# Expert loop of a routed layer: branch hints for TensorE, and the second tile behind the third and later ones

## Chip, cores and metric

The kernel runs on one core of one Trainium2 chip. The metric is the device time of one execution in microseconds (us). TensorE (PE) multiplies; its weight loads are listed as PEld, and the profile puts the steps of its sequencer there too, as PEldq. VectorE is DVE, ScalarE ACT, GpSimd POOL, SyncE SP.

## The reference

Three layers follow each other on 3072 tokens: an attention with a window of 16 and block sums, a dense gated layer `((x @ w1) * (x @ w2)) @ w3 @ w_out`, and a routed layer, which the change is about:

```python
skip_score = x @ w_skip
do_compute = skip_score > 0
out = x.copy()
xc = x[do_compute]
logits = xc @ w_gate                       # 8 experts
e_idx = np.argmax(logits, axis=1)
gate_w = probs[np.arange(len(xc)), e_idx]  # softmax of the chosen one
for e in range(E):
    mask = e_idx == e
    h = np.maximum(xc[mask] @ w1[e], 0.0)  # 512 x 1024
    y[mask] = gate_w[mask, None] * (h @ w2[e])
out[do_compute] = xc + y
```

How many tokens an expert gets is known only at run time. The inputs here give experts 0 to 7 the counts 266, 41, 394, 201, 29, 63, 212 and 100.

## The kernel before

Attention and the dense layer fill the span up to about 655 us, and the router writes, beside them, a list of token numbers for each expert and the number of tiles of 128 tokens. The expert stage then runs `Experts.run` (L845): the experts are unrolled in the program, and for each the number of tiles `ns[e]` decides by branches which of its code is run. All five engines carry the same branches; the order inside a block is the order in which the code is written.

One tile is `compute` (L765): 24 matmuls for the hidden layer (`hmul`, two halves of 12), relu on ScalarE, eight transposes (`hturn`), 24 matmuls for the output (`ymul`), a scaling and addition on VectorE (`eo`) and a scatter on GpSimd. Products are made from a high and a low part of each operand, so a tile's rows have to be gathered (`gather`, GpSimd), turned by TensorE (`turn`, four transposes) and split by ScalarE (`xh`, high) and VectorE (`xl`, low) before `hmul` can start. This is done ahead, inside the tile before: the argument `turns` names the slots that are turned in the middle of the tile, ahead of its last 12 matmuls, and at its end. Slots 0 and 2 take the first tile of the even and the odd experts by turns, 1 and 3 the second (`own`), 4 the third, 5 the fourth; `nxt` is the next expert's first. In the trace the slots' buffers are all named xg, exh and exl; the order of instructions keeps numbers: xg_7303, 7307, 8648, 8652, 8656 and 8660 are slots 0 to 5.

Inside `compute`, `other()` also casts pieces of the next expert's weights (`piece`: high part on ScalarE, L734, low part on VectorE, L737), 16 pieces an expert: `HALF` spreads 8 over a tile, `CUTS` 16. The pieces come from seven buffers (eraw); when one is free, SyncE loads the next 512 KB into it (L718).

An expert with more than one tile goes through the true part of `tc.If(ns[e] > 1)`: first and second tile (`second`), then `rest`, which is nested: a third tile if there are more than two, a fourth if more than three, a loop for any further one. Where a branch is not taken, a short block makes up for the counts of the semaphores that the skipped code would have raised; on TensorE it waits until all earlier matmuls are done. An expert with one tile goes through the else part. The code of each part stands in this order: first and second tile, third, fourth, loop, those short blocks, else part; a jump leads over what is not run. Expert 0's first tile is ahead of its branch, and expert 7 has no else part.

Of the kernel before, what the change touches and what calls it, by code (L numbers as in the profile page):

```python
# [52 lines left out]
PE = ET.PE  # L53
PIECES = "a"
RMORE = 3
CUTS0 = (0, 1, 1, 1, 2, 3)
ELOAD = 16
CUTS = (4, 3, 1, 2, 3, 3)
HALF = (2, 1, 0, 1, 2, 2)
# [3 lines left out]
class Attention:  # L63
# [60 lines left out]
    def sum(self, i):  # L124
        nc = self.nc
        vt = self.sums.pop(i)
        sm = self.pool.tile([4 * NBLK, D], F32, tag="sm", name="sm", bufs=2)
        for n in (8, 4, 2):
            nc.vector.tensor_add(vt[:, 0:n, :], vt[:, 0:n, :], vt[:, n : 2 * n, :])
        nc.vector.tensor_add(sm, vt[:, 0, :], vt[:, 1, :])  # L130
        self.sums["half", i] = sm
        if i % 2:
            nc.vector.tensor_add(sm, self.sums.pop(("half", i - 1)), self.sums.pop(("half", i)))
            nc.vector.tensor_scalar_mul(self.vs[:, i // 4, i // 2 % 2, :], sm, 1.0 / 32.0)
# [225 lines left out]
def split(nc, hi, lo, src):  # L360
    nc.scalar.activation(hi, src, AF.Copy)
    nc.vector.tensor_sub(lo, src, hi.bitcast(F32))  # L362
# [309 lines left out]
class Experts:  # L672
# [92 lines left out]
    def compute(self, col, e, slot, turns=(None, None), cuts=()):  # L765
        nc, pool, ps = self.nc, self.pool, self.ps
        (ah, al), (bh, bl) = self.a[e % 2], self.b[e % 2]
        xg, xh, xl = self.xg[slot], self.xh[slot], self.xl[slot]
        hrs, ths = [], []
        hps = [ps.tile([P, 512], F32, tag="h", name="hp", bufs=2) for _ in range(2)]  # L770
        cuts = list(cuts)

        def other():
            for _ in range(cuts.pop(0) if cuts else 0):
                self.piece(PIECES)

        def hmul(s, lo, hi):
            fs = slice(s * 512, s * 512 + 512)
            for q in range(lo, hi):
                c, j = divmod(q, 3)  # L780
                l, r = ((xh, ah), (xh, al), (xl, ah))[j]
                nc.tensor.matmul(hps[s], l[:, c, :], r[c][:, fs], start=(q == 0), stop=(q == 11))  # L782

        def relu(s):
            hr = pool.tile([P, 512], F32, tag="hr", name="hr", bufs=2)
            nc.scalar.activation(hr, hps[s], AF.Relu)  # L786
            hrs.append(hr)

        def hturn(s):
            tp = ps.tile([P, 4, P], F32, tag="ht", name="htp", bufs=2)  # L790
            for c in range(4):
                nc.tensor.transpose(tp[:, c, :], hrs[s][:, c * P : (c + 1) * P], self.ident)
            th = pool.tile([P, 4, P], F32R, tag="th", name="hth", bufs=2)
            tl = pool.tile([P, 4, P], F32R, tag="tl", name="htl", bufs=2)
            split(nc, th, tl, tp)
            ths.append((th, tl))

        yp = ps.tile([P, 512], F32, tag="y", name="yp", bufs=2)

        def ymul(s, lo, hi):  # L800
            th, tl = ths[s]
            for q in range(lo, hi):
                c, j = divmod(q, 3)
                f = 4 * s + c
                l, r = ((th, bh), (th, bl), (tl, bh))[j]
                nc.tensor.matmul(
                    yp, l[:, c, :], r[f], start=(f == 0 and j == 0), stop=(f == 7 and j == 2)
                )

        hmul(0, 0, 12)  # L810
        other()
        relu(0)
        hmul(1, 0, 6)
        other()
        hturn(0)
        other()
        hmul(1, 6, 12)
        relu(1)
        if turns[0] is not None:
            self.turn(turns[0], ps)  # L820
        other()
        ymul(0, 0, 6)
        hturn(1)
        other()
        ymul(0, 6, 12)
        if turns[1] is not None:
            self.turn(turns[1], ps)
        other()
        ymul(1, 0, 12)
        if turns[2:]:  # L830
            self.turn(turns[2], ps)
        o = pool.tile([P, DM], F32, tag="o", name="eo", bufs=2)
        nc.vector.scalar_tensor_tensor(
            out=o, in0=yp, scalar=xg[:, DM : DM + 1], in1=xg[:, 0:DM], op0=ALU.mult, op1=ALU.add
        )
        nc.gpsimd.indirect_dma_start(  # L836
            out=self.out,
            out_offset=bass.IndirectOffsetOnAxis(ap=col, axis=0),
            in_=o,
            in_offset=None,  # L840
            bounds_check=N - 1,
            oob_is_err=False,
        )

    def run(self, pool, ps, early):  # L845
        tc, nc = self.tc, self.nc
        self.pool, self.ps = pool, ps
        cj = pool.tile([P, 1], I32, name="cj")
        manual = lambda: tc.manual_schedule(engines=ENGINES)
        with tc.If(early < P):  # L850
            with manual():
                self.gather(self.col(0, 0), 0)
                self.turn(0, ps)
        with tc.If(early < 2 * P):
            with manual():
                self.gather(self.col(0, 1), 1)
        def state():
            return self.done, self.loaded, dict(self.raws), list(self.free)

        def rest(e, p):  # L860

            with tc.If(ns[e] > 2):  # L862
                with manual():
                    self.compute(self.col(e, 2), e, 4, (5, None))
                with tc.If(ns[e] > 3):  # L865
                    with manual():
                        self.compute(self.col(e, 3), e, 5)
                    with tc.If(ns[e] > 4):  # L868
                        with tc.For_i(4, ns[e], 1) as j:
                            nc.vector.tensor_copy(cj, self.idx[:, bass.ds(j + e * NTILE, 1)])  # L870
                            self.gather(cj, 4)
                            self.turn(4, ps)
                            self.compute(cj, e, 4)

        def second(e, p, cuts=()):
            self.gather(self.col(e, 3), 5)
            self.compute(self.col(e, 1), e, (1, 3)[p], (4, None), cuts)

        ns = None
        for e in range(E):  # L880
            p = e % 2
            more = e + 1 < E
            own, nxt = (1, 3)[p], (2, 0)[p] if more else None
            with manual():
                if more:
                    self.gather(self.col(e + 1, 0), (2, 0)[p])
                self.gather(self.col(e, 2), 4)
                if more:
                    self.gather(self.col(e + 1, 1), (3, 1)[p])
                if e == 0:  # L890
                    self.compute(self.col(0, 0), 0, 0, (None, 1, nxt), CUTS0)
                elif not more:
                    self.compute(self.col(e, 0), e, (0, 2)[p], (own, None))
            if ns is None:
                ns = [nc.values_load(self.nt[0:1, z : z + 1], min_val=0, max_val=NTILE) for z in range(E)]  # L895
            if not more:
                with tc.If(ns[e] > 1):
                    with manual():
                        second(e, p)
                    rest(e, p)  # L900
                continue


            before = state()
            with tc.If(ns[e] > 1) as many:  # L905
                with manual():
                    if e:
                        self.compute(self.col(e, 0), e, (0, 2)[p], (own, nxt), HALF)
                    second(e, p, HALF)
                rest(e, p)  # L910
            after = state()
            self.done, self.loaded, self.raws, self.free = before[0], before[1], dict(before[2]), list(before[3])
            with many.Else():
                with manual():
                    if e:
                        self.compute(self.col(e, 0), e, (0, 2)[p], (None, nxt), CUTS)
                    else:
                        for _ in range(sum(HALF)):
                            self.piece(PIECES)
            now = state()  # L920
            assert now[:2] == after[:2] and list(now[2]) == list(after[2])
            assert [id(t) for t in now[3]] == [id(t) for t in after[3]]
# [251 lines left out]
```

## Time and profile before

| | |
|---|---|
| median of 3 runs | 875.9 us (875.15 to 879.59) |
| profiled execution | 877.2 us |
| its span, first to last instruction | 875.4 us |
| TensorE busy in the span | 821.2 us (94%) |
| VectorE, ScalarE, GpSimd busy | 513.4, 466.0, 99.3 us |
| mean granted clock of TensorE | 0.984 |
| packets of the instruction fetch (queue q8) | 64, together 1.05 MB |

The span is cut into 40 slices of 21.9 us; the expert stage fills the last ten. [...] An idle time in brackets stands ahead of an instruction and names what ended it; "issue" is a wait for nothing that the profile shows. It is counted from the end of the instruction before, which is modelled for matmuls. Branches, loads of a register and event waits of a sequencer are not counted as busy time, but have their own rows by source line.

### The profile page before, as it was taken

The page shows a single profiled execution, that of the slowest core. Times are in us where ns is not written, and L with a number is a line of the kernel's source. Part 1 is how long each engine was busy: PE and PEld are TensorE (multiplying, and loading weights), DVE is VectorE, ACT ScalarE, POOL GpSimd, SP SyncE. Part 2 cuts the span into 40 slices and gives each one's busy share as a digit, 9 for nine tenths or more (in the row PEclk, how much of TensorE's full clock was granted, in tenths as well). Part 3 has the DMA queues.
Part 4 walks back from the last instruction along what each step waited for, and adds up shares of the span by engine and source line. Part 5 has one row for each costly group of instructions (what it writes and reads, how often), then busy time and mean ns, then how long its engine had stood idle before and what let it go on. Part 6 is the DMA issues. An engine that isn't in the chain of part 4 may idle for free. (4 is left out here: it accounts for less than half of the span.)

```text
span 875.4 us, 17512 instructions
## 1 busy us (share of the span) xinstructions
PE 821.2 (94%) x6478; PEld 766.4 (88%) x6478; DVE 513.4 (59%) x1663; ACT 466.0 (53%) x1230; POOL 99.3 (11%) x135
## 2 busy tenths in 40 slices
PE   3988889999999999999999999999999799996996
PEld 3988879999999999999999998999998687784684
DVE  5888888876555546457535456633435365254861
ACT  5777988775663444455434446522426364254761
POOL 2000000000001100010001000210214121022321
PEclk9999999999999999999999999999999999997999
DMA  7959965542522423215212212710326376045920
GB/s 209 236 168 207 225 167 174 148 100 59 130 56 74 116 73 89 57 35 123 73 37 62 58 49 67 242 50 1 104 96 245 111 225 209 13 137 166 306 80 21
DMA packets 124612, 105.02 MB, mean 120 GB/s; under 512 B 92914, under 2 KB 98082, under 8 KB 124496
## 3 DMA queue, kind: packets, MB, share of 16 engines
q1 hardware_dynamic: 120144, 98.04, 40.2%
q0 software_dynamic: 4352, 5.51, 2.1%
q8 instruction: 64, 1.05, 0.5%
q14 instruction: 52, 0.43, 0.2%
HBM read 90.45 MB, written 16.64 MB: 122 GB/s over the span
## 5 line engine op out<-in xcount | busy, mean ns | idle before, releaser
L547 PE MATMUL x2p<-wh,slab 128*128 128x266 f32 (+1 forms) x768 | 156.1, 290 | 0.0
L547 PEld LDWEIGHTS x2p<-wh,slab 128*128 128x128 f32 x768 | 124.2, 189 | 0.8
L547 PE MATMUL x2p<-wl,slab 128*128 128x256 f32 (+1 forms) x384 | 108.9, 284 | 0.0
L200 ACT ACTIVATE pr<-pr,st 128x120 f32<-128x120 f32 x192 | 73.4, 384 | 34.5 <-DVE st L190 34.2
L526 DVE TENSOR_TENSOR a<-a,ab 128x256 f32<-128x256 f32 x84 | 35.2, 419 | 76.5 <-ACT a L517 76.0
L504 PE MATMUL ab<-slab,wA1h 128*128 128x256 f32 x384 | 72.4, 286 | 0.5 <-DVE slab L362 0.5
L547 PEld LDWEIGHTS x2p<-wl,slab 128*128 128x128 f32 x384 | 72.8, 190 | 0.0
L504 PE MATMUL ab<-slab,wB1h 128*128 128x256 f32 x384 | 72.5, 287 | 0.0
L517 ACT ACTIVATE a<-ab 128x256 f32<-128x256 f32 x96 | 36.3, 378 | 65.7 <-PE ab L504 62.0
L504 PE MATMUL ab<-slab,wB2h 128*128 128x256 f32 x384 | 70.7, 282 | 0.0
L504 PE MATMUL ab<-slab,wA2h 128*128 128x256 f32 x384 | 70.6, 282 | 0.0
L527 ACT ACTIVATE slab<-a 128x256 fp32r<-128x256 f32 x84 | 35.0, 417 | 63.6 <-DVE a L526 63.1
L504 PEld LDWEIGHTS ab<-slab,wA1h 128*128 128x128 f32 x384 | 59.0, 189 | 1.1 <-DVE slab L362 0.7
L504 PEld LDWEIGHTS ab<-slab,wB1h 128*128 128x128 f32 x384 | 58.9, 190 | 0.4
L504 PEld LDWEIGHTS ab<-slab,wB2h 128*128 128x128 f32 x384 | 59.1, 190 | 0.0
L504 PEld LDWEIGHTS ab<-slab,wA2h 128*128 128x128 f32 x384 | 59.1, 189 | 0.0
L528 DVE TENSOR_TENSOR slab<-a,slab 128x256 fp32r<-128x256 f32 x84 | 36.1, 430 | 38.7 <-ACT slab L527 38.2
L178 PE MATMUL sp<-kaug,qblk 128*128 128x120 f32 x384 | 53.1, 284 | 4.6 <-issue 2.9
L786 ACT ACTIVATE hr<-hp 128x512 f32<-128x512 f32 x30 | 17.9, 598 | 71.1 <-PE hp L782 71.0
L504 PE MATMUL ab<-slab,wA2l 128*128 128x256 f32 x192 | 54.1, 282 | 0.0
L504 PE MATMUL ab<-slab,wA1l 128*128 128x256 f32 x192 | 54.1, 282 | 0.0
L504 PE MATMUL ab<-slab,wB2l 128*128 128x256 f32 x192 | 53.9, 281 | 0.0
(178 smaller groups left out, 2134.5 us busy)
## 6 DMA issues: line engine op xcount, KB each, us to landing
eraw<-in_moe_w SPq DMA_DIRECT2D x64, 512.0 KB
raw<-in_moe_w SPq DMA_DIRECT2D x32, 512.0 KB
vaug<-in_v SPq DMA_DIRECT2D x32, 240.0 KB
x2e<-row SPq DMA_DIRECT2D x24, 256.5 KB
vt<-in_v SPq DMA_DIRECT2D x16, 384.0 KB
kn<-in_k SPq DMA_DIRECT2D x32, 192.0 KB
qn<-in_q SPq DMA_DIRECT2D x32, 192.0 KB
out<-row SPq DMA_DIRECT2D x24, 256.0 KB
```

The costliest lines, as they stand in the source:

```text
L178: self.nc.tensor.matmul(sp[:, i, 0:KA], self.qblk[:, t, :, :], self.kaug[:, t, :], start=True, stop=True)
L200: nc.scalar.activation(pr[:, i, :], pr[:, i, :], AF.Exp, scale=-1.0, bias=st[:, 0, i : i + 1], accum_out=st[:, 1, i : i + 1],)
L504: self.nc.tensor.matmul(pp[:, s, :], l[:, c, fs], r[:, c, :], start=(c == 0 and j == 0), stop=(c == 3 and j == 2),)
L517: nc.scalar.activation(a, pp[:, 0, :], AF.Copy)
L526: nc.vector.tensor_mul(a, a, pp[:, 1, :])
L527: nc.scalar.activation(gh[:, f % 4, :], a, AF.Copy)
L528: nc.vector.tensor_sub(gl[:, f % 4, :], a, gh[:, f % 4, :].bitcast(F32))
L547: self.nc.tensor.matmul(po[:, 0 : hi - lo], l[:, f, s * P : s * P + P], r[:, 4 * h + f, lo:hi], start=(h == 0 and f == 0 and j == 0), stop ...
L786: nc.scalar.activation(hr, hps[s], AF.Relu)
```

## The change

Three things change. First, four branches of each expert carry labels, and `soon` places a hint on TensorE (a register step that compares `ns`, and the hint) at the start of a tile: at the start of the first tile for the branch behind it, at the third for the next, at the fourth for the next, and at an expert's last tile for the first branch of the next expert. For expert 0 the hint for its second branch stands right ahead of that branch. Second, in the true part the second tile is computed behind `rest`, hence after the third and later ones; slot 4 is turned in the first tile already (for experts 1 to 7 in the place of the next expert's turn, which moves to the tile's end; for expert 0 at the very end), and the gather of the fourth tile comes ahead of the first. Third, expert 7 gets the same form as the others, with an else part.

```diff
--- before.py
+++ after.py
@@ -827,8 +827,9 @@
             self.turn(turns[1], ps)
         other()
         ymul(1, 0, 12)
-        if turns[2:]:
-            self.turn(turns[2], ps)
+        for slot in turns[2:]:
+            if slot is not None:
+                self.turn(slot, ps)
         o = pool.tile([P, DM], F32, tag="o", name="eo", bufs=2)
         nc.vector.scalar_tensor_tensor(
             out=o, in0=yp, scalar=xg[:, DM : DM + 1], in1=xg[:, 0:DM], op0=ALU.mult, op1=ALU.add
@@ -857,24 +858,26 @@
         def state():
             return self.done, self.loaded, dict(self.raws), list(self.free)
-        def rest(e, p):
-
-            with tc.If(ns[e] > 2):
+        def soon(label, n, least):
+
+            tc.mark_branch_hint_location(label, hint=n >= least, engines=[PE])
+
+        def rest(e):
+
+            with tc.If(ns[e] > 2, label=f"three{e}"):
                 with manual():
+                    soon(f"four{e}", ns[e], 4)
                     self.compute(self.col(e, 2), e, 4, (5, None))
-                with tc.If(ns[e] > 3):
+                with tc.If(ns[e] > 3, label=f"four{e}"):
                     with manual():
+                        soon(f"five{e}", ns[e], 5)
                         self.compute(self.col(e, 3), e, 5)
-                    with tc.If(ns[e] > 4):
+                    with tc.If(ns[e] > 4, label=f"five{e}"):
                         with tc.For_i(4, ns[e], 1) as j:
                             nc.vector.tensor_copy(cj, self.idx[:, bass.ds(j + e * NTILE, 1)])
                             self.gather(cj, 4)
                             self.turn(4, ps)
                             self.compute(cj, e, 4)
-
-        def second(e, p, cuts=()):
-            self.gather(self.col(e, 3), 5)
-            self.compute(self.col(e, 1), e, (1, 3)[p], (4, None), cuts)
         ns = None
         for e in range(E):
@@ -888,32 +891,33 @@
                 if more:
                     self.gather(self.col(e + 1, 1), (3, 1)[p])
                 if e == 0:
-                    self.compute(self.col(0, 0), 0, 0, (None, 1, nxt), CUTS0)
-                elif not more:
-                    self.compute(self.col(e, 0), e, (0, 2)[p], (own, None))
+                    self.compute(self.col(0, 0), 0, 0, (None, 1, nxt, 4), CUTS0)
             if ns is None:
                 ns = [nc.values_load(self.nt[0:1, z : z + 1], min_val=0, max_val=NTILE) for z in range(E)]
-            if not more:
-                with tc.If(ns[e] > 1):
-                    with manual():
-                        second(e, p)
-                    rest(e, p)
-                continue
+            half, whole = (HALF, CUTS) if more else ((), ())
+
             before = state()
-            with tc.If(ns[e] > 1) as many:
+            with tc.If(ns[e] > 1, label=f"two{e}") as many:
                 with manual():
+                    soon(f"three{e}", ns[e], 3)
+                    self.gather(self.col(e, 3), 5)
                     if e:
-                        self.compute(self.col(e, 0), e, (0, 2)[p], (own, nxt), HALF)
-                    second(e, p, HALF)
-                rest(e, p)
+                        self.compute(self.col(e, 0), e, (0, 2)[p], (own, 4, nxt), half)
+                rest(e)
+                with manual():
+                    if more:
+                        soon(f"two{e + 1}", ns[e + 1], 2)
+                    self.compute(self.col(e, 1), e, own, (None, None), half)
             after = state()
             self.done, self.loaded, self.raws, self.free = before[0], before[1], dict(before[2]), list(before[3])
             with many.Else():
                 with manual():
+                    if more:
+                        soon(f"two{e + 1}", ns[e + 1], 2)
                     if e:
-                        self.compute(self.col(e, 0), e, (0, 2)[p], (None, nxt), CUTS)
+                        self.compute(self.col(e, 0), e, (0, 2)[p], (None, nxt), whole)
                     else:
                         for _ in range(sum(HALF)):
                             self.piece(PIECES)
```

Expert 0's branches on TensorE; xg_8648 is the next expert's first tile, xg_8656 and exh_8657 the third tile's slot 4 (a piece of the difference):

```order
 L762 MATMUL xt<-ident,xg_8648 128x128 x4
-L895 TENSOR_LOAD nt
-L905 COMPARE_AND_BRANCH
+L762 MATMUL xt<-ident,xg_8656 128x128 x4
+L896 TENSOR_LOAD nt x2
+L902 COMPARE_AND_BRANCH
+L863 REGISTER_ALU
+L1174 BRANCH_PREFETCH_HINT
+L867 COMPARE_AND_BRANCH
+L863 REGISTER_ALU
+L1174 BRANCH_PREFETCH_HINT
+L782 MATMUL hp<-ea0h,exh_8657 128x512
```

The turn of slot 4 has moved to the end of the first tile, and behind the two branches the third tile comes first.

TensorE from expert 0's last tile to expert 1's first, before; L868, L865 and L862 are the short blocks of the branches not taken, exh_8649 is expert 1's first tile:

```order
L868 UNCONDITIONAL_BRANCH
L865 UNCONDITIONAL_BRANCH
L862 UNCONDITIONAL_BRANCH
L905 UNCONDITIONAL_BRANCH
L895 TENSOR_LOAD nt
L905 COMPARE_AND_BRANCH
L782 MATMUL hp<-ea1h,exh_8649 128x512
```

The same place after the change, first up to the second tile of expert 0 (exh_7308):

```order
L875 UNCONDITIONAL_BRANCH
L871 UNCONDITIONAL_BRANCH
L867 UNCONDITIONAL_BRANCH
L863 REGISTER_ALU
L1174 BRANCH_PREFETCH_HINT
L782 MATMUL hp<-ea0h,exh_7308 128x512
```

and, behind that tile's matmuls, up to expert 1's first:

```order
L902 UNCONDITIONAL_BRANCH
L863 REGISTER_ALU
L1174 BRANCH_PREFETCH_HINT
L902 UNCONDITIONAL_BRANCH
L896 TENSOR_LOAD nt
L902 COMPARE_AND_BRANCH
L863 REGISTER_ALU
L1174 BRANCH_PREFETCH_HINT
L782 MATMUL hp<-ea1h,exh_8649 128x512
```

The second tile now stands between the short blocks and the next expert's branch.

ScalarE at the start of expert 1's true part, as it is for all experts from 1 to 6, before; ea0h is the next expert's first weight, hr the relu:

```order
L905 COMPARE_AND_BRANCH
L734 ACTIVATE ea0h<-eraw_7312 128x512 x2
L786 ACTIVATE hr<-hp 128x512
L734 ACTIVATE ea0h<-eraw_7313 128x512
L361 ACTIVATE hth<-htp 128x512
```

and after, where wA1h belongs to the next expert's second weight:

```order
L902 COMPARE_AND_BRANCH
L734 ACTIVATE ea0h<-eraw_7312 128x512 x2
L734 ACTIVATE wA1h<-eraw_8665 128x512 x2
L786 ACTIVATE hr<-hp 128x512
L734 ACTIVATE ea0h<-eraw_7313 128x512
L361 ACTIVATE hth<-htp 128x512
```

Two casts of the second weight, which stood in the second tile, have moved ahead of the first tile's relu.

## Rows read from the trace of the kernel before

**Rows 1.** The page: granted clock of TensorE in 40 slices, in tenths.
```profile
PEclk9999999999999999999999999999999999997999
```
**Rows 2.** Timeline of TensorE: start, duration (us), engine, line, operation, count [idle before].
```profile
681.32 0.39 PE L782 MATMUL hp<-ea0h,exh 128*128 128x512 f32 x1
...
698.30 0.77 PE L782 MATMUL hp<-ea1h,exh 128*128 128x512 f32 x1 [4.38 <-issue]
...
765.25 0.49 PE L782 MATMUL hp<-ea1h,exh 128*128 128x512 f32 x1 [1.03 <-ACT ea0h L734]
...
798.45 0.77 PE L782 MATMUL hp<-ea0h,exh 128*128 128x512 f32 x1 [7.48 <-issue]
...
815.21 0.47 PE L782 MATMUL hp<-ea1h,exh 128*128 128x512 f32 x1 [1.47 <-ACT ea0h L734]
...
855.54 0.50 PE L782 MATMUL hp<-ea1h,exh 128*128 128x512 f32 x1 [1.05 <-PEq L862]
```
**Rows 3.** TensorE's sequencer by source line, cut by stretches: count, ns min/median/max, first and last start.
```profile
L905 PEldq COMPARE_BRANCH  x1: 3377/3377/3377, 694.8 to 694.8; - x1
L868 PEldq COMPARE_BRANCH  x2: 181/264/347, 761.5 to 764.5; - x2
L868 PEldq EVENT_SEMAPHORE  x1: 51/51/51, 764.3 to 764.3; - x1
L895 PEldq TENSOR_LOAD <-nt x1: 302/302/302, 764.7 to 764.7; - x1
L862 PEldq COMPARE_BRANCH  x2: 181/2190/4199, 788.2 to 792.7; - x2
L905 PEldq COMPARE_BRANCH  x1: 4988/4988/4988, 793.3 to 793.3; - x1
L905 PEldq COMPARE_BRANCH  x1: 4012/4012/4012, 811.0 to 811.0; - x1
L862 PEldq COMPARE_BRANCH  x2: 193/1764/3334, 851.7 to 855.3; - x2
```
**Rows 4.** Queue q8: packets, MB, share; whole span, 788.2 to 798.3, 713.7 to 764.
```profile
q8 instruction: 64, 1.05, 0.5%
q8 instruction: 3, 0.05, 2.2%
q8 instruction: 3, 0.05, 0.4%
```
**Rows 5.** Stretches: us, PE, PEld, DVE, ACT, POOL busy, granted clock, DMA share, GB/s.
```profile
655.80:660.09 4.29, 4.29 (x18) 3.43 (x19) 0.00 (x0) 1.12 (x2) 2.94 (x5) 1.00 0.35 126
698.30:705.28 6.98, 6.98 (x18) 5.46 (x19) 0.58 (x2) 1.43 (x3) 2.06 (x2) 0.57 0.61 191
798.45:804.91 6.46, 6.46 (x18) 5.05 (x19) 0.00 (x0) 1.14 (x3) 0.00 (x0) 0.63 0.23 80
```
**Rows 6.** Timeline, all engines, end of expert 0's first tile.
```profile
668.38 0.60 PE L762 MATMUL xt<-ident,xg 128*128 128x128 f32 x4
668.74 0.48 PE L782 MATMUL hp<-ea0h,exh 128*128 128x512 f32 x1
669.02 0.60 ACT L361 ACTIVATE exh<-xt 128x512 fp32r<-128x512 f32 x1 [1.07 <-PE xt L762]
669.65 0.69 DVE L362 TENSOR_TENSOR exl<-xt,exh 128x512 fp32r<-128x512 f32 x1 [0.72 <-ACT exh L361]
```
**Rows 7.** Timeline of GpSimd and TensorE, expert 2's first tile: gather of slot 4, next expert's turn.
```profile
719.19 1.00 POOL L749 DMA_INDIRECT xg<-x2e,idx  x1 [0.30 <-issue]
723.76 0.66 PE L762 MATMUL xt<-ident,xg 128*128 128x128 f32 x4 [0.23 <-DMA xg<-x2e,idx]
```
**Rows 8.** Expert 5's tile: VectorE's busy time, granted clock; and SyncE's loads around it.
```profile
815.21:828.89 13.68, 11.43 (x20) 1.00 0.93 317
809.47 22.20 SPq L718 DMA_DIRECT2D eraw<-in_moe_w  x13
```

## The prediction

> **What bounds the kernel now.** I read the page first: TensorE's granted clock is 0.9 or more in every slice of the span but one, near 790 to 810 us [rows 1]. Its timeline then shows why: TensorE stands still there. In the expert stage (15 tiles; the inputs give experts 0 to 7 the counts 3, 1, 4, 2, 1, 1, 2, 1) it is fed almost without a break inside a tile, and its timeline has five seams between experts, with the idle time in brackets [rows 2]: 4.38 us before expert 1, 1.03 before expert 3, 7.48 before 4, 1.47 before 5, 1.05 before 7. Together 15.4 us; only this can be won.
>
> What ends these waits is TensorE's own sequencer [rows 3]. A short jump (at 761.5, over the unused loop of expert 2) takes 0.35 us. The long ones take 3.38 us (694.8, into expert 1's else part), 4.20 (788.2, over expert 3's unused tiles), 4.99 (793.3, into expert 4's else part), 4.01 (811.0, expert 5's) and 3.33 (851.7, over expert 6's unused tiles). While two of them run, from 788.2 to 798.3, the queue of the instruction fetch moves three packets; 64 of them make 1.05 MB, so one is 16 KB [rows 4]. A long jump waits for code.
>
> Part of such a wait is hidden. The sequencer reached the jump at 811.0, and TensorE ran dry at 815.21 - 1.47 = 813.74: a lead of 2.7 us. Before experts 1 and 4 the lead was lost for a second reason. After a branch not taken, the sequencer waits until TensorE is empty (the event at 764.3, where the last matmul's end is 765.25 - 1.03 = 764.22), and the next long jump comes only then, with nothing left to hide it.
>
> The two long seams cost more than their idle time [rows 5]. [...] Expert 5, after 1.47 us of idling, kept full clock [rows 8].
>
> **Part by part: what is removed.** Each long jump that is taken now has a hint one tile earlier, that is some 12.5 us ahead of a fetch of 3.3 to 5.0. And the second tile now stands behind the branches of the third and later ones, so that the emptying of TensorE comes inside an expert, and the jump into the next expert has its lead back. If the hints fetch as they say, the five seams go: 15.4 us. The idle times that remain are of the size of expert 5's, which left the clock alone, so 2.69 + 2.17 = 4.9 us go with them. Expert 7 loses the turn of its unused second tile (the else part asks for none): a turn in the stream takes 668.74 - 668.38 = 0.36 us [rows 6]. Sum 20.7.
>
> **What is added or moved.**
> Emptying: experts 0, 2, 3 and 6 have two or more tiles and leave the branches early, so four times TensorE empties ahead of the second tile. The nearest row is the seam before expert 3, whose jump was short: 1.03 us. Of that the load of the count, 0.30, moves away, behind the second tile, where the lead hides it; the next compare goes with it, a register step and a hint come instead, which I take as equal, since no hint runs in the trace of before. So 0.73 each, 2.9 in all. Lowest: the event 0.08 after the end, the branch 0.2 later, 0.18 for it, that is 0.46 or 1.8 for four. Highest: the seam before expert 7, 1.05, or 4.2.
> Expert 0's third tile: its turn (slot 4) is now the last thing ahead of the tile that needs it. The turn before it shows the chain: transposes at 668.38, cast on ScalarE from 669.02, subtraction on VectorE from 669.65 to 670.34 [rows 6]. The new turn follows 0.36 us later, and each step waits for the one ahead, some 0.6 further: the low part is ready at about 670.95. The third matmul would want it 0.54 after the tile's start at 668.74 + 0.36, at 669.64. That is 1.3, with the hand-over 1.4; bounds 0.9 and 2.3, the latter if the gather is late as well.
> Slot 4's turn in the others stands where the next expert's stood, which at expert 2 waited for its gather (0.23 from the modelled end); slot 4's gather is issued right behind that one, and an issue takes 1.0 us [rows 7]. I take 0.7 at expert 2 and nothing at 3 and 6, whose third gathers hold no rows; bounds 0 and 1.7.
> One-tile experts: 1, 4 and 5 cast 16 pieces of weights in one tile, and in the idle time before 1 and 4 these casts ran ahead. Expert 5 had little such time: it lasted 13.68 us [rows 8], against 681.32 - 668.74 = 12.58 for another tile with one turn [rows 2, 6], with VectorE busy for 11.4 of it. I take 0.3 more for each of 1 and 4; bounds 0 and 1.1 each.
> Two casts of the second weight move ahead of the first tile's relu in experts with several tiles, as the order on ScalarE shows. They need a load that is issued late in the expert before; SyncE issued 13 loads in 22.2 us, 1.7 each [rows 8]. Behind a one-tile expert (at 2 and 6) such a load may land 1.5 to 2 us into the tile, and the relu is due after 12 of those 18 matmuls, at 2.9: I take 0.5 in all; bounds 0 and 2.5.
> At nothing: the other register steps, hints and count loads, hidden by the lead of 2.7 us (0.3 a load if it is gone); the gather of the fourth tile, moved ahead of a scatter on GpSimd and due a tile later; GpSimd's step at the join, moved inside the expert, where that queue waits for VectorE anyway.
> Sum 2.9 + 1.4 + 0.7 + 0.6 + 0.5 = 6.1; bounds 2.7 and 12.9.
>
> Net: 20.7 - 6.1 = 14.6 us, from 7.8 to 18.0. The profiled execution took 877.2 us (span 875.4) and would take 862.6. It lies 1.3 above the median of 875.9, so the forecast is 861.3, from 857.9 to 868.1.
>
> **Rivals.**
> Hints that fetch nothing. For: no hint runs in the trace of before. Against: only the purpose of the instruction. The reorder still keeps the leads. Over the forecast stay 3.38 - 2.7 = 0.7 (into expert 1), 1.4 (over expert 3's tiles: done at 792.4, dry at 790.97), 4.99 - 2.7 = 2.3 (into 4), 1.5 (into 5, as before), 0.5 (over expert 6's: 855.03 against 854.49) and 1.5 (into 7, taken like 5): 7.9 us, so 869.2.
> Hints that push out code (slower). A hinted line could take the place of the line that follows in sequence. From 713.7 to 764, four tiles in a row, three packets of code were fetched [rows 4], so a hint and its branch, a tile apart, straddle a boundary rather more often than every second time: four of the seven long jumps. Each would stall in mid-tile, where there is no lead, for at least the 3.4 us of a jump, and the hinted line be lost as well: 869.2 + 4 x 3.4 = 882.8. It is slower by more than the noise from stalls of 11.1 us in all on (880.3 - 869.2), 2.8 each. For: the longest jump, 4.99, came right behind another. [...]
> [...]
> Weights late. If the moved casts, the one-tile experts and slot 4's gather cost their upper bounds (2.5 + 2.2 + 1.7 against 1.8), it is 861.3 + 4.6 = 865.9.
>
> **How the numbers follow.** Forecast 0.72, weights late 0.08, idle hints 0.13, code pushed out 0.07. A measurement can tell about 0.5% from no change: 871.5 to 880.3. The first two lie below that, idle hints (869.2) a little more than half of the time, pushed-out code mostly above it. Faster 0.87, same 0.08, slower 0.05. The range takes in the forecast's bounds and most of the idle hints: 858 to 870.
>
> **What would show it.** In the trace after: jumps of TensorE's sequencer near 0.35 us in place of 3.3 to 5.0; no low clock behind expert 0 and expert 3; four gaps of 0.5 to 1.1 us ahead of the second tile of experts 0, 2, 3 and 6; about 1.4 us in expert 0 before its third tile; experts 1, 4 and 5 at about 13 us. Jumps still of 3 to 5 us mean idle hints. Idle time in mid-tile that nothing but the sequencer ends means code pushed out. TensorE waiting for relu or casts at the start of experts 2 and 6 means late weights.

## The result, and the profile after

The changed kernel takes 865.7 us (median of 4 runs, 864.11 to 866.77), the kernel before beside it 877.8 (875.15 to 879.62): ratio 0.9863, 95% interval 0.9827 to 0.99. It is 12.1 us faster. The forecast was 861.3 with a range of 858 to 870. The profiled execution took 864.1 us, with a span of 862.3. In two of the runs further down one of ten executions took far longer than the rest (1137.4 and 2007.5 us) and is left out of the ratio, so only the lowest time stands beside the median there.

The page of the changed kernel, the row that answers to [rows 1]; the slice near 800 us has its clock back:

```profile
PEclk9999999999999999999999999999999999999999
```

TensorE's timeline after (columns as in [rows 2]), at the starts of tiles and at the waits inside them:

```profile
667.79 0.48 PE L782 MATMUL hp<-ea0h,exh 128*128 128x512 f32 x1 [0.76 <-ACT exh L361]
...
676.62 1.09 PE L762 MATMUL xt<-ident,xg 128*128 128x128 f32 x4 [2.25 <-DMA xg<-x2e,idx]
...
685.40 0.49 PE L782 MATMUL hp<-ea0h,exh 128*128 128x512 f32 x1 [0.64 <-PEq L871]
...
697.56 0.40 PE L782 MATMUL hp<-ea1h,exh 128*128 128x512 f32 x1
...
721.76 0.66 PE L762 MATMUL xt<-ident,xg 128*128 128x128 f32 x4 [1.40 <-DMA xg<-x2e,idx]
...
777.33 0.50 PE L782 MATMUL hp<-ea1h,exh 128*128 128x512 f32 x1 [0.73 <-ACTq L867]
...
789.50 0.39 PE L782 MATMUL hp<-ea0h,exh 128*128 128x512 f32 x1
...
814.52 0.63 PE L762 MATMUL xt<-ident,xg 128*128 128x128 f32 x4 [2.32 <-DMA xg<-x2e,idx]
```

Experts 1 (697.56) and 4 (789.50) start without a bracket where [rows 2] had 4.38 and 7.48. What is left is of two kinds: the emptying ahead of a second tile (0.64 at 685.40, 0.73 at 777.33, and 0.73 each at 750.89 and 832.07), and three waits of the turn (L762) for a gather: 2.25 in expert 0's third tile, 1.40 in expert 2's first, 2.32 in expert 5's.

TensorE's sequencer, as in [rows 3]: over the third tile (L867) of experts 3 and 6, into the next expert (L902; of two records the second is the jump of interest, the first a jump over the else part):

```profile
L902 PEldq COMPARE_BRANCH  x2: 195/268/342, 695.0 to 695.7; - x2
L867 PEldq COMPARE_BRANCH  x1: 348/348/348, 773.2 to 773.2; - x1
L902 PEldq COMPARE_BRANCH  x2: 213/280/347, 787.0 to 787.7; - x2
L902 PEldq COMPARE_BRANCH  x1: 350/350/350, 799.8 to 799.8; - x1
L867 PEldq COMPARE_BRANCH  x1: 346/346/346, 827.9 to 827.9; - x1
L902 PEldq COMPARE_BRANCH  x2: 202/264/326, 841.7 to 842.0; - x2
```

All are at 0.33 to 0.35 us; before, they were 3.3 to 5.0.

Stretches (columns as in [rows 5]). First the expert stage of the kernel before, then of the changed one the whole stage, the starts of experts 1 and 4, and the matmuls behind the gather wait of 2.25:

```profile
655.80:868.33 212.53, 196.14 (x912) 156.79 (x912) 111.58 (x174) 103.66 (x190) 49.23 (x45) 0.96 0.47 155
```

```profile
653.41:856.48 203.07, 193.11 (x908) 153.97 (x908) 110.98 (x173) 103.34 (x189) 49.22 (x45) 0.99 0.48 163
697.56:704.54 6.98, 6.88 (x32) 5.31 (x31) 6.02 (x10) 4.66 (x10) 3.16 (x3) 1.00 0.85 273
789.50:795.96 6.46, 6.46 (x31) 5.08 (x29) 5.51 (x9) 4.18 (x9) 4.21 (x4) 1.00 0.85 262
676.62:680.12 3.50, 3.50 (x12) 2.92 (x13) 0.69 (x1) 0.60 (x1) 0.00 (x0) 0.54 0.00 0
```

The stage lost 9.5 us in this pair of executions: 212.53 to 203.07. TensorE's idle time in it fell by 6.4 (16.4 to 10.0) and its busy time by 3.0 (196.1 to 193.1), since the low clock of [rows 5] is gone. Between the last matmul and the end of the span lay 7.1 us before and 5.8 after: the kernel before had one more long jump there, over expert 7's unused tiles.

```profile
L897 PEldq COMPARE_BRANCH  x1: 3899/3899/3899, 866.0 to 866.0; - x1
```

The rest of the difference of the two spans is an earlier start of the stage (653.41 against 655.80). It lies ahead of the change and differs from execution to execution (653.2 to 658.8 in the other runs with the changed order).

### The profile page after: what moved, and what is told of

It is laid out like the page before. It is cut to its first block, busy times and chain, and to the rows that moved or that the text cites. A ratio compares the mean times of both kernels' runs of the same rounds, so it can differ in the third digit from the quotient of the medians.

```text
span 862.3 us, 17536 instructions
## 1 busy us (share of the span) xinstructions
PE 817.4 (95%) x6474; PEld 762.6 (88%) x6474; DVE 512.9 (59%) x1662; ACT 465.3 (54%) x1229; POOL 98.4 (11%) x135
## 5 line engine op out<-in xcount | busy, mean ns | idle before, releaser
L504 PE MATMUL ab<-slab,wB1l 128*128 128x256 f32 x192 | 53.9, 281 | 0.0
```

Of the source, the lines that this page charges most:

```text
L504: self.nc.tensor.matmul(pp[:, s, :], l[:, c, fs], r[:, c, :], start=(c == 0 and j == 0), stop=(c == 3 and j == 2),)
```

## The experiments

The first question was which half of the change brings the gain, and whether the hints fetch at all.

**Order without hints.** `soon` does nothing; all else as in the changed kernel.

```diff
-            tc.mark_branch_hint_location(label, hint=n >= least, engines=[PE])
+            return
```

> The changed kernel without its hints; the new order of tiles stays. If the hints fetch the code (theory), the long jumps of TensorE's sequencer are back at 3.3 to 5.0 us, partly hidden by a lead of 2.7 us, and the time is 7.9 us above the changed kernel: about 873.6 us. If the order alone brings the gain (rival), it stays at 865 to 867 us.

Measured: 870.6 us (866.63 to 873.81), ratio 0.991, interval 0.9877 to 0.9942. The sequencer, in the order of the rows of after above:

```profile
L902 PEldq COMPARE_BRANCH  x2: 168/2050/3933, 694.6 to 695.2; - x2
L867 PEldq COMPARE_BRANCH  x1: 337/337/337, 775.4 to 775.4; - x1
L902 PEldq COMPARE_BRANCH  x2: 169/1928/3686, 789.3 to 790.0; - x2
L902 PEldq COMPARE_BRANCH  x1: 5337/5337/5337, 805.8 to 805.8; - x1
L867 PEldq COMPARE_BRANCH  x1: 329/329/329, 836.0 to 836.0; - x1
```

The jumps into experts 1, 4 and 5 (and 7, 3.3) are long again, where the changed kernel had 0.33 to 0.35 us: the hints do fetch (there one packet of code moved from 776.9 to 787 us, between the hint for expert 4 and its branch). But the jumps over the third tiles of 3 and 6 are short without any hint, while [rows 3] had 4.2 and 3.3 for them. That I had not expected. The idle time left into 1, 4, 5 and 7 is 2.06, 1.81, 2.79 and 1.42, since the lead hides the rest. The time is 3 us under the 873.6 that were expected.

**Hints that point the wrong way.** The comparison in `soon` is reversed, so each hint names the way that is not taken; this is for the rival that hints push out code.

```diff
-            tc.mark_branch_hint_location(label, hint=n >= least, engines=[PE])
+            tc.mark_branch_hint_location(label, hint=n < least, engines=[PE])
```

> The changed kernel with each hint turned round, so that it names the side that is not taken. If a hinted line takes the place of the line that follows in sequence (rival named before), expert 2, whose branches fall through three times, shows idle time of TensorE in mid-tile that only its sequencer ends, and the time lies clearly above the kernel without hints, by 3 us for each such stall (880 us or more). If a hinted line has its own place (theory), it is as without hints: about 873.6 us, and expert 2 runs as in the changed kernel.

Measured: 873.4 us (869.26 to 877.9), ratio 0.996, interval 0.9931 to 0.9989. The jumps into 1, 4, 5 and 7 took 3.6, 3.6, 4.8 and 3.3 us, much as without hints. Here all code stands where it stands in the changed kernel, since only the comparison differs; so the place of the code is not what made these four jumps short there, the right hint is. The jumps over the third tiles of 3 and 6 are short again (0.36 and 0.34), with a wrong hint. The median is 2.8 us above that of the run without hints; the intervals overlap, and the profiled executions are alike (spans of 871.5 and 872.0). All brackets of TensorE from 713 to 767 us (expert 2, four tiles in a row):

```profile
725.21 0.66 PE L762 MATMUL xt<-ident,xg 128*128 128x128 f32 x4 [1.52 <-DMA xg<-x2e,idx]
...
754.22 0.49 PE L782 MATMUL hp<-ea0h,exh 128*128 128x512 f32 x1 [0.61 <-PEq L875]
```

A gather and the emptying, nothing in mid-tile that the sequencer ends. But in expert 2 the fetch queue moved three packets, as in [rows 4] and in the changed kernel, so the wrong hints brought no further code there that could have pushed any out. One more packet came in expert 1's tile (one from 704 to 712 us, where the run without hints has none from 704 to 716), and TensorE shows no wait from 699.11 to 725.21. Wrong hints are useless here, and the stalls that the rival forecast are nowhere in the stage: it falls for this kernel.

**Hints without the order.** The kernel before, with its own order and all hints, those for three and for the next expert both at the second tile's start.

```diff
         def second(e, p, cuts=()):
+            soon(f"three{e}", ns[e], 3)
+            if e + 1 < E:
+                soon(f"two{e + 1}", ns[e + 1], 2)
             self.gather(self.col(e, 3), 5)
```

> The kernel before with the hints alone: its order of tiles, gathers and turns stays. Theory (both parts needed): TensorE empties at the seam between experts as before, so four seams of about 1.0 us stay, but the fetches (15 us of jumps) go; no new wait for a gather comes. By the rows of before that is 15.4 - 4.2 of idle time and 4.9 of low clock, 16.1 us below the kernel before, about 861.5 us, which is faster than the changed kernel, because the new order costs 5.2 us of new waits for gathers and 0.8 for a turn. Rival (the new order is what saves the leads): the seams before experts 1 and 4 keep 2 us or more and the time is at or above the changed kernel's 865.7 us.

Measured: 875.0 us (871.39 to 879.27), ratio 0.997, interval 0.9948 to 0.9992: next to nothing, against my expectation. The jump into expert 1 (L914), over expert 3's third tile (L866), into experts 4 and 5:

```profile
L914 PEldq COMPARE_BRANCH  x1: 3325/3325/3325, 695.7 to 695.7; - x1
L866 PEldq COMPARE_BRANCH  x2: 208/2248/4287, 788.8 to 793.3; - x2
L914 PEldq COMPARE_BRANCH  x1: 2756/2756/2756, 794.0 to 794.0; - x1
L914 PEldq COMPARE_BRANCH  x1: 355/355/355, 809.1 to 809.1; - x1
```

The hint for expert 5, which stands alone in expert 4's tile, worked (4.0 before). Those for expert 1's branch and for the third tiles of 3 and 6 were followed by another hint before their branch came, the one for expert 4 by a long jump. So the next run keeps one kind alone.

**The old order with one hint at a time.** The run before, without the hints for three, four and five.

```diff
         def second(e, p, cuts=()):
-            soon(f"three{e}", ns[e], 3)
             if e + 1 < E:
                 soon(f"two{e + 1}", ns[e + 1], 2)
```

> The kernel before, in its own order, with only one kind of hint: the next expert's branch, given at the start of the second tile (or in place of it); no hint for the third, fourth and fifth tile. Theory (TensorE keeps one hint, and a later one displaces it): the jump into expert 1 falls from 3.3 to 0.35 us and brings back the low clock behind it, the jump into expert 4 falls from 2.8 to 0.35, into 5 and 7 they stay at 0.35; the jumps over the third tiles of experts 3 and 6, which have no hint, keep 4.2 and 3.3 us. Time some 9 us under the kernel before, ratio 0.988 to 0.992. If a jump that misses discards the hint given ahead of it, the jump into 4 stays at 2.8 and the ratio is near 0.993. Rival (it was not the displaced hint but the old order itself in which hints come to nothing): as in the run of the old order with all hints, 0.997, with the jump into expert 1 still over 3 us.

Measured: 871.6 us (from 868.97; 10 runs), ratio 0.9946, interval 0.9917 to 0.9974. The same three jumps, and the one into expert 5; then the jump over expert 6's third tile and, a tile later, the one over expert 7's unused tiles (L903, which was L897 before):

```profile
L911 PEldq COMPARE_BRANCH  x1: 347/347/347, 694.9 to 694.9; - x1
L866 PEldq COMPARE_BRANCH  x2: 201/2192/4184, 782.9 to 787.3; - x2
L911 PEldq COMPARE_BRANCH  x1: 4215/4215/4215, 787.9 to 787.9; - x1
L911 PEldq COMPARE_BRANCH  x1: 385/385/385, 804.2 to 804.2; - x1
L866 PEldq COMPARE_BRANCH  x2: 209/1770/3331, 846.7 to 850.2; - x2
L903 PEldq COMPARE_BRANCH  x1: 377/377/377, 860.6 to 860.6; - x1
```

The jump into expert 1 falls from 3.3 to 0.35 as soon as no other hint follows the one for it: here the later hint undid the earlier one. And the hint for expert 4 is lost although none followed; between it and its branch lay the long jump over expert 3's third tile. The rival of that expectation falls. Its second branch (a jump that misses costs the hint) is not shown: the hint for expert 7, given at 833.9, had the long jump of 3.33 us at 846.7 behind it, and its own jump still took 0.38 in place of 3.90; in the run before it was 0.37, behind one of 3.86. For expert 4 the fetch queue moved no packet between 767 and 784 us, so that nothing had been fetched for the hint of 770.0 when the long jump began at 782.9. There the next branch followed right behind the long jump, at expert 7 a whole tile later. Which of this decides stays open; the jump into 4 took 4.2 us and not the 2.8 of the run before.

**Only the hints into the next expert, in the new order.**

```diff
-                    soon(f"four{e}", ns[e], 4)
...
-                        soon(f"five{e}", ns[e], 5)
...
-                    soon(f"three{e}", ns[e], 3)
```

> The changed kernel without the hints for the third, fourth and fifth tile; the hint for the next expert's branch stays. Theory (the jumps over the third tiles of experts 3 and 6 took 0.34 and 0.33 us in the run without hints too, so only the jumps into the next expert need one): the same time as the changed kernel within 0.3%, and jumps of 0.33 to 0.38 everywhere. Rival (each hint carries its own share): the jumps over the third tiles of 3 and 6 take over 3 us again, 6 us more than the changed kernel.

Measured: 865.3 us (862.7 to 870.58), ratio 0.9889, interval 0.9818 to 0.9959, with the changed kernel beside it at 865.6. Over the third tile (L867) and into the next expert (L900), whole stage, the longest of four and of twelve:

```profile
L867 PEldq COMPARE_BRANCH  x4: 65/205/347, 666.7 to 827.7; - x4
L900 PEldq COMPARE_BRANCH  x12: 73/206/367, 666.5 to 841.8; - x12
```

The other three hints carry nothing here. The changed kernel beside it, once more:

> The changed kernel once more, as the mark for the runs beside it on one chip: ratio 0.983 to 0.990, a stage of the experts of 203 us, gather waits of 6 us in three places.

It gave 865.6 us (863.43 to 867.92), ratio 0.9872, interval 0.9809 to 0.9935; its stage took 200.5 us.

**The hint right ahead of its branch.** As the run with one kind of hint, but each at its tile's end.

```diff
-                        soon(f"two{e + 1}", ns[e + 1], 2)
                     self.compute(self.col(e, 1), e, own, (None, None), half)
+                    if more:
+                        soon(f"two{e + 1}", ns[e + 1], 2)
```

> The changed kernel with only the hints for the next expert's branch, and those given at the end of the tile ahead of the branch in place of its start: in TensorE's program the hint stands right ahead of the branch. Theory (the fetch takes 3.3 to 5.3 us and TensorE's sequencer runs only some 2 us ahead of its matmuls): most of each miss stays, jumps of 3 us and more, the time that of the run without hints, ratio 0.990 to 0.992. Rival (the lead does not matter, a hint is answered at once): jumps of 0.35, ratio 0.986 as the changed kernel.

Measured: 872.2 us (from 869.35; 10 runs), ratio 0.9954, interval 0.9925 to 0.9983: no better than without hints (0.991), and a little worse than expected; the two intervals overlap. The jumps into 1, 4, 5 and 7 took 3.1, 3.5, 4.4 and 3.0 us. That is 0.2 to 0.9 us less than without hints: a hint without lead saved nothing worth the name here.

**The same kernels with the code moved.** Why were the jumps over third tiles short without hints? Either by where their code stands, or by the order, in which the second tile follows the jump. Expert 0's loop for a fifth tile gets one more tile's code. It does not run here; everything behind it only stands 112 instruction places further on (a tile's 56 matmuls with a weight load each). Had the order decided, both jumps would stay at 0.33 to 0.36 us. Once with only the hints into the next expert:

```diff
                             self.compute(cj, e, 4)
+                            if e == 0:
+                                self.compute(cj, e, 4)
```

> The changed kernel with only the hints for the next expert's branch, and with one more tile's code in expert 0's loop for a fifth tile and further ones, which does not run (expert 0 has three tiles). [...]

Measured: 872.3 us (867.88 to 874.99), ratio 0.9935, interval 0.9909 to 0.9961. Over the third tile, whole stage, and into expert 4:

```profile
L867 PEldq COMPARE_BRANCH  x4: 65/1706/4272, 668.2 to 831.4; - x4
L902 PEldq COMPARE_BRANCH  x2: 337/1998/3658, 786.3 to 787.1; - x2
```

And once with all hints of the changed kernel:

> The changed kernel with all its hints and with the same code that does not run in expert 0. Theory (the hint for the third tile's branch is what the changed kernel needs where its code stands badly): jumps of 0.33 to 0.38 us everywhere, the time of the changed kernel, ratio 0.986. Rival (the hint at the first tile's start comes to nothing, as in the old order): the jumps over the third tiles of 3 and 6 take over 3 us, ratio 0.989 to 0.993.

Measured: 871.3 us (868.09 to 872.64), ratio 0.9922, interval 0.9891 to 0.9953. The same two rows (L904 is its line for the next expert's branch):

```profile
L867 PEldq COMPARE_BRANCH  x4: 73/214/348, 670.1 to 831.7; - x4
L904 PEldq COMPARE_BRANCH  x2: 336/2040/3743, 788.1 to 789.0; - x2
```

For the third tiles the place decides: code that never runs makes these jumps 4.27 and 3.34 us long, and their own hints then bring them back to 0.35. But in both runs the hinted jumps into experts 4 and 7 are long too (3.7 and 3.1 with all hints), with no second hint and no long jump between hint and branch. What marks them is the short jump over the else part just ahead: 0.31 to 0.34 us, against 0.20 where the hint worked. The fetch queue tells a little more: with all hints it moved no packet from 778 to 789, between the hint for expert 4 and its branch, and none from 836 to 845 for expert 7, while the changed kernel moved one from 776.9 to 787. So nothing was fetched for these hints; why stays open. Which places make a jump long is not shown by these runs either, only that a move of 112 places did.

**The gathers ahead.** The three gathers that TensorE waits for are issued earlier: in expert 0 ahead of the first tile, else in the expert before, ahead of its last scatter (`third` gathers slot 4 of the next expert, `first` the first tile of the expert after it).

```diff
+                if e == 0:
+                    self.gather(self.col(e, 2), 4)
...
+                    self.gather(self.col(e, 3), 5)
...
-                    self.compute(self.col(0, 0), 0, 0, (None, 1, nxt, 4), CUTS0)
+                    self.compute(self.col(0, 0), 0, 0, (None, 1, 4, nxt), CUTS0)
...
                         soon(f"two{e + 1}", ns[e + 1], 2)
+                    third()
+                    first()
```

> The changed kernel with the gathers issued earlier on GpSimd: the fourth tile's of expert 0 ahead of its first tile, the third tile's and the next expert's first in the expert before, ahead of its last scatter; in expert 0 the third tile is turned ahead of the next expert's. If the waits for gathers in the changed kernel's trace (2.25, 1.40 and 2.32 us) and the wait for the turn in expert 0 (0.76) are on the path (theory), 6 us go: about 859.5 us. If loads of weights hold the gathers whatever their place in the queue (rival), the waits stay and the time is 865 us.

Measured: 863.2 us (860.67 to 863.9), ratio 0.9832, interval 0.9805 to 0.986. The stage, and the waits of the turn that are left in it:

```profile
655.21:852.76 197.55, 191.52 (x908) 152.83 (x908) 111.22 (x173) 103.29 (x189) 50.35 (x45) 1.00 0.49 167
```

```profile
718.62 0.63 PE L762 MATMUL xt<-ident,xg 128*128 128x128 f32 x4 [0.78 <-DMA out<-eo,idx]
...
810.01 0.63 PE L762 MATMUL xt<-ident,xg 128*128 128x128 f32 x4 [0.98 <-issue]
```

1.8 us in place of 6.0; expert 0's is gone, and 0.52 of the 0.76 ahead of its third tile is left. The forecast of 859.5 was 3.7 us too low: it counted on the waits of one execution, and they come to 5.0 and 3.8 in the two other profiled ones of the changed kernel. At expert 6 TensorE waits a new 0.59 for ScalarE's relu, which stands behind two casts that waited 2.67 for a load: here weights come next.

**Where it ends.** Both together: the gathers ahead, and only the hints into the next expert; beside it the changed kernel.

> The version in which the experiments end: the changed kernel with the earlier gathers of the run before, and only the hints for the next expert's branch. Theory (the gathers that TensorE waits for come to under 2 us, the hints for the third, fourth and fifth tile carry nothing): as the run with the earlier gathers, ratio 0.981 to 0.986, a stage of the experts of 197 to 199 us with under 6.5 us of idle time. Rival (the gathers move the wait only, to SyncE's weights or to a later gather): a stage of 201 to 203 us as the changed kernel, ratio 0.986.

> The changed kernel beside it on one chip, as the mark: ratio 0.984 to 0.989, a stage of the experts of 200 to 203 us, gather waits of 4 to 6 us in three places. Rival: none, it is what the run beside it is held against.

Measured: 862.1 us (857.93 to 864.7), ratio 0.9827, interval 0.9791 to 0.9863, against 864.5 (863.0 to 866.3) and 0.9864, interval 0.9833 to 0.9895. Their stages, this version first:

```profile
657.18:854.23 197.05, 191.61 (x908) 152.86 (x908) 111.28 (x173) 103.26 (x189) 50.41 (x45) 1.00 0.50 168
```

```profile
656.01:855.41 199.40, 191.55 (x908) 152.84 (x908) 111.06 (x173) 103.42 (x189) 49.47 (x45) 1.00 0.49 166
```

The whole of the 2.4 us is idle time (7.9 to 5.4 of the stage); the medians differ by the same amount, though the two intervals overlap.

## Why the prediction was right, and where not

**The five seams, 15.4.** Right in size: all five are gone from the timeline. The reason given was half right. The hints make the jumps into the next expert short (0.33 to 0.35 us, without them 3.3 to 5.3). The jumps over the third tiles of 3 and 6 became short because the code now stands elsewhere, which was luck; in the moved code (4.27 and 3.34 without their hints, 0.35 with them) they needed their hints.

**The low clock, 4.9.** Right: 1.00 at the starts of experts 1 and 4, where [rows 5] had 0.57 and 0.63. The two terms are differences of [rows 5] for the same 18 matmuls: 6.98 - 4.29 and 6.46 - 4.29. In the trace of before the first 13 matmuls of expert 1 (698.30 to 703.98) and the first 11 of expert 4 (798.45 to 803.20) had a granted clock of 0.50. But the changed kernel lowered the clock somewhere else: 0.54 for the 12 matmuls behind the wait of 2.25 us. From the first transpose of the turn to the end of the six matmuls of `ymul` behind it (676.62 to 680.12) the engine took 3.50 us, against 2.03 in the execution beside the last version, which waited 1.04 and kept its clock (0.39 to 0.47 us for each of the six matmuls, against 0.48 to 0.78): 1.5 more.

**Emptying, 4 x 0.73 = 2.9.** Measured 0.64 and three times 0.73, 2.83. The price read from the seam ahead of expert 3, less the load of the count, was good to a tenth. But at experts 3 and 6 the last to come was ScalarE's step of the same branch (at 777.3, when TensorE's sequencer had given its hint at 776.9), which the prediction's chain does not have; so the agreement there is in part chance.

**Expert 0's late turn, 1.4.** Measured 0.76 ahead of the third tile, and its first 18 matmuls took 4.76 us where the others take 4.4: together 1.1.

**Gathers, 0.7: the step that was mis-sized.** The waits came to 6.0 us against 0.8 before, so 5.2. In other executions of the changed kernel they were 5.0 and 3.8. Three parts:
- Expert 2's slot 4, the only one in the sum: 1.40 in place of 0.7.
- Expert 0's slot 5, costed "at nothing ... due a tile later": 2.25. In expert 0 the third tile now follows the first directly, and in its middle slot 5 is turned; the tile in between, which was the slack, has moved behind. And the gather is not ahead of a scatter there, since expert 0's first tile stands ahead of the branch. GpSimd, after:

```profile
669.48 1.21 POOL L837 DMA_INDIRECT out<-eo,idx  x1 [5.68 <-DVE eo L834]
671.00 1.03 POOL L749 DMA_INDIRECT xg<-x2e,idx  x1 [0.30 <-issue]
672.33 1.00 POOL L749 DMA_INDIRECT xg<-x2e,idx  x1 [0.30 <-issue]
```

  The scatter waits for the tile's end, one more gather goes first, and slot 5's is issued at 672.33. TensorE wants it at 676.62 - 2.25 = 674.37, 2.0 us later; it is there 4.3 us after its issue.
- Expert 5's next turn, 2.32, which the prediction left as it was (0.55 before). With the seams gone the same chain of scatter and gather has less time: in the runs without hints and with reversed ones, where the seam into 5 was 2.79 and 2.44, this wait is absent.

The edit on GpSimd was read as an order of instructions and not as a date by which each gather is due. The run with the gathers ahead shows the term: stage 197.6 us against 199.4 to 203.1 in three profiled executions of the changed kernel.

**One-tile experts and moved casts, 1.1.** Not seen. Experts 1 and 4 took 12.87 and 12.91 us for their tile, and no bracket of the changed kernel names a cast of weights or a relu. (The upper bound of 1.1, from expert 5's 13.68, held that tile's wait for a gather, 0.55.) The wait that was forecast for late weights appears in two other runs: 0.59 at expert 6 with the gathers ahead, and 0.98 at expert 2 in the run with all hints and the code moved, where the wait for the gather is absent.

**The sum.** Removed 15.4 + 4.9 + 0.4 (expert 7's turn: 908 matmuls in place of 912). Added 2.8 (emptying), 1.1 (turn), 5.2 (gathers) and, in this execution, 1.5 of low clock behind the gather: 10.6. Net 10.1, against 9.5 measured in the stage; the 1.3 at the kernel's end, which the prediction did not count, come on top. Medians: 12.1 in place of 14.6. The 865.7 us lie on the price of the rival "weights late" (865.9), but its cause was not that.

**The rivals.** Idle hints: the run without hints put them at 870.6 where 869.2 was worked out; the parts differ, with no wait over the third tiles, 2.06 in place of 0.7 into expert 1 and 2.79 in place of 1.5 into 5, so that the sums lie so close is partly chance. Code pushed out: no such stall with the reversed hints. (Its seven long jumps are six in the rows: the five of [rows 3] and the 3.90 over expert 7's unused tiles.) In expert 0's second tile, between its start at 685.40 and the jump at 695.7, the fetch queue moved one packet and no other; how many pieces of code are held at once no run shows.

## What to carry to other kernels

A hint for a long jump worked here (0.35 us in place of 3.3 to 5.3) when no other hint stood between it and its branch and it came a tile ahead, and even then not everywhere: order alone gave a ratio of 0.991, hints alone 0.9946 at best and 0.997 at worst, both together 0.9863. Hint the jumps that the trace shows to be long in the code as built, and look at the jump times again after every edit that shifts code, even code that does not run: 112 places took back about half of this gain. When a reorder takes the slack between two tiles, list for every gather the time when it can be issued and the time when it is due; three waits for gathers cost 5.2 us in the profiled execution, nearly as much as all else that was added (5.4).

## What the runs showed of the hardware that was not expected

- **One hint.** In the old order, with a second hint given behind it, the hint for expert 1 came to nothing (jump of 3.3 us, 0.35 without the second). The hint for expert 4 there came to nothing with a long jump between it and a branch right behind that jump (4.2), the one for expert 7, with a tile between the two, did not (0.38). In the moved code the hints for experts 4 and 7, ahead of short jumps of 0.31 to 0.34 us, came to nothing as well (3.7 and 3.1 with all hints). In three of these places (expert 4 in the old order, experts 4 and 7 in the moved code with all hints) no packet of code moved between the hint and its branch or the long jump; why is open.
- **Place of the code.** The same jump over expert 3's third tile, without a hint for it, took 0.34 us in the run without hints and 4.27 with the code moved.
- **Clock.** In the run without hints the 18 matmuls behind idle times of 1.81 and 2.79 us ran at a lower clock (0.72), those behind 2.06 did not (1.00; each row takes in two to four transposes more):

```profile
699.32:703.75 4.43, 4.43 (x20) 3.57 (x21) 1.90 (x4) 1.29 (x3) 2.18 (x3) 1.00 0.93 283
793.83:799.99 6.16, 6.16 (x22) 4.90 (x23) 2.36 (x5) 1.49 (x3) 3.44 (x4) 0.72 0.90 273
811.26:817.43 6.17, 6.17 (x22) 4.90 (x23) 1.59 (x4) 1.49 (x3) 5.17 (x4) 0.72 0.86 305
```

  In the moved code with all hints a wait of 2.56 us for a gather (expert 5, 818.36) left the matmuls behind it at 0.39 to 0.48 us each; with only the hints into the next expert, those behind one of 2.65 (816.50) took 0.59 to 0.78 for the first seven. So the length of the wait by itself did not decide here, and what did stays open; where the clock fell in the run without hints, the 18 matmuls took 1.5 us more each time (5.98 against 4.44).
